# Inverse root by Ln and Exp on ScalarE, held weight transfers and deeper input buffers in an attention kernel

## The chip, the cores and the metric

The kernel runs on one core of a Trainium2 chip. The metric is the device time of one execution in microseconds. A core has five instruction streams that work side by side: TensorE (PE), VectorE (DVE), ScalarE (ACT), GpSimd (POOL) and SyncE (SP), each in the order of its own queue; transfers run on 16 DMA engines. Weight loads into TensorE have a row of their own in the profile (PEld), and "SPq" is SP's queue of transfers.

## The reference

Attention with normalised queries and keys over 8 batches, 12 heads, 448 positions and 64 channels, and then a two-layer network on the 3584 tokens:

```python
def rmsnorm(x, g):
    rms = np.sqrt(np.mean(x * x, axis=-1, keepdims=True) + 1e-06)
    return x / rms * g
q_n, k_n = (rmsnorm(q, g_q), rmsnorm(k, g_k))
scores = 1.0 / np.sqrt(64) * np.matmul(q_n, k_n.transpose(0, 1, 3, 2))
attn = softmax(scores)              # exp of (scores - max), over (sum + 1e-09)
x = np.matmul(attn, v)              # heads side by side: 3584 x 768
h = x @ w_in                        # 768 x 2048
out = (h * np.clip(h + 3.0, 0.0, 6.0) / 6.0) @ w_out    # 2048 x 768
```

## The kernel before

**Tiling.** A *pair* is two heads of one batch: 6 pairs per batch, 48 in all, counted by `P`. Of the 448 positions, 384 lie as three rows on each of 128 partitions (the pair's tiles); the other 64, the *rest rows*, are handled for all heads and two batches at once.

**One pair.** `load_pair` (L133) issues three transfers on SP: q and k into `qk` (L138), v into `vf` (L141). `prep_pair` (L146) makes the normalised rows on POOL: the squares `sq` (L150), their sums by 64 on DVE (`ssq`, L152), then `rstd_of` (L126): `ms`, mean plus epsilon (L128), and `rs`, that to the power -0.5 against a constant tile (L130). Two products give `qks` (L158) and a cast of v gives `va` (L164). `trans_pair` (L235) transposes `qks` on PE (L241), DVE copies q out to `qT` (L243) and k times the gains to `kp` (L247). `score` (L253) does one matmul and one exponential on ACT (`eT`, L264) per unit, seven per pair; `av` (L279) multiplies by the values, and DVE divides by the sum (`rd`, `xn`, L289, L291); `xtrans` (L324) transposes back. `load_rest`, `load_vrest`, `prep_rest` and `prep_vrest` (L170 to L208) do the same for the rest rows: `qkr` (L174), `vr` (L183), `vbd` (L190, POOL), `sqr` (L200), `qkrs` (L205). The scores of a batch need its rest rows, since `qT` holds all 448 positions.

**The network.** `h_part` (L341) multiplies by `w_in` (L349), ACT makes `t_sb` = relu(h/6 + 0.5) (L354), DVE takes min(t, 1) times h as `gT` (L356). `y_part` (L360) multiplies by `w_out` (L366), ACT copies to `y_sb` (L372), SP stores (L376, L380).

**Order.** The last loop (L464) merges the attention of batch b with the first layer of batch b-1 and the second layer of batch b-2; what is left of the network follows. Inside `att_items(P)` (L436) come the load of pair P+4, the preparation of P+3, the transposes of P+2, the scores of P+1 and the values of P. At the start (L449 to L462) four pairs are loaded, POOL issues the transfers of `w_in` (L452), three pairs are prepared, POOL issues those of `w_out` (L456), and the first scores follow. These positions are priorities: a planner in the framework simulates the engines, takes for each the ready instruction of highest priority and so fixes each queue's order beforehand; on the chip a queue then keeps that order. In the trace the squares of a pair stand several pairs ahead of its `qks`. A buffer is a limit to running ahead: four of `qk`, three of `vf`, four each of `ssq`, `ms`, `rs` and `qks`, two of `sq`, one of `qkr` (L99 to L104). A load into a `qk` buffer waits until the `qks` of the pair that held it is made; one into `vf`, for the cast.

Of the kernel before, what the change touches and what calls it, by code (L numbers as in the profile page):

```python
# [12 lines left out]
A_ADD = mybir.AluOpType.add  # L13
A_POW = mybir.AluOpType.pow
A_MIN = mybir.AluOpType.min
EXP = mybir.ActivationFunctionType.Exp
RELU = mybir.ActivationFunctionType.Relu
# [5 lines left out]
def kernel(  # L23
# [35 lines left out]
    for a in range(2):  # L59
        nc.sync.dma_start(out=gq_t[a * 64:(a + 1) * 64, :], in_=g_q.rearrange("(p o) -> p o", o=1))  # L60
        nc.sync.dma_start(out=gk_t[a * 64:(a + 1) * 64, :], in_=g_k.rearrange("(p o) -> p o", o=1))
    mask = const.tile([128, 2], FP32, name="mask")
# [5 lines left out]
    gmask = const.tile([128, 2], FP32, name="gmask")  # L68
    nc.vector.tensor_scalar(gmask[:], mask[:], gprime[:], 1.0 / 8.0, A_MULT, A_MULT)
    half_c = const.tile([128, 1], FP32, name="half_c")  # L70
    nc.gpsimd.memset(half_c[:], 0.5)
    zero_c = const.tile([128, 1], FP32, name="zero_c")
    nc.gpsimd.memset(zero_c[:], 0.0)
    npow = const.tile([128, 24], FP32, name="npow")
    nc.gpsimd.memset(npow[:], -0.5)

# [21 lines left out]

    qk_pool = pool("qk_pool", 4)  # L99
    v_pool = pool("v_pool", 3)  # L100
    sq_pool = pool("sq_pool", 2)
# [21 lines left out]
    st = {}  # L123


    def rstd_of(ssq, n):  # L126
        ms = st_pool.tile([128, n], FP32, name="ms", tag="ms")
        nc.gpsimd.tensor_scalar(ms[:], ssq, 1.0 / D, 1e-6, A_MULT, A_ADD)  # L128
        rs = st_pool.tile([128, n], FP32, name="rs", tag="rs")
        nc.gpsimd.tensor_tensor(out=rs[:], in0=ms[:], in1=npow[:, 0:n], op=A_POW)  # L130
        return rs

    def load_pair(P):  # L133
# [12 lines left out]
    def prep_pair(P):  # L146
        qk, vf = st.pop(("qk", P)), st.pop(("vf", P))
        sq = sq_pool.tile([128, 4 * NT * D], FP32, name="sq", tag="sq")
        qk_flat = qk[:].rearrange("p a h x -> p (a h x)")
        nc.gpsimd.tensor_tensor(out=sq[:], in0=qk_flat, in1=qk_flat, op=A_MULT)  # L150
        ssq = st_pool.tile([128, 4 * NT], FP32, name="ssq", tag="ssq")
        nc.vector.tensor_reduce(  # L152
            out=ssq[:], in_=sq[:].rearrange("p (n d) -> p n d", d=D), axis=AX_X, op=A_ADD)
        rs = rstd_of(ssq[:], 4 * NT)
        rs4 = rs[:].rearrange("p (a h t) -> p a h t", a=2, h=2)
        qks = qks_pool.tile([128, 2, NT, 2, D], BF16, name="qks")
        for i in range(2):
            nc.gpsimd.tensor_tensor(  # L158
                out=qks[:, i].rearrange("p t h d -> p h t d"),
                in0=qk[:, i].rearrange("p h (t d) -> p h t d", d=D),  # L160
                in1=rs4[:, i].unsqueeze(3).to_broadcast([128, 2, NT, D]),
                op=A_MULT)
        va = va_ring[P % NVA]
        nc.gpsimd.tensor_copy(  # L164
            out=va[:, :, :, 0:D], in_=vf[:].rearrange("p h (t d) -> p h t d", d=D))
        st["qks", P] = qks
        st["va", P] = va


    def load_rest(b):  # L170
        qkr = rst_pool.tile([128, 2, H, D], FP32, name="qkr")
        for i, src in enumerate((q, k)):
            for e in range(2):
                nc.sync.dma_start(  # L174
                    out=qkr[e * 64:(e + 1) * 64, i],
                    in_=src[b + e, :, SM:S, :].rearrange("h p d -> p h d"))
        st["qkr", b] = qkr
# [16 lines left out]
    def prep_rest(b):  # L194
        qkr = st.pop(("qkr", b))
        qks = rst_pool.tile([128, 2, H, D], BF16, name="qkrs")
        for i in range(2):
            sq = sq_pool.tile([128, 4 * NT * D], FP32, name="sqr", tag="sq")
            src = qkr[:, i].rearrange("p h d -> p (h d)")
            nc.gpsimd.tensor_tensor(out=sq[:], in0=src, in1=src, op=A_MULT)  # L200
            ssq = st_pool.tile([128, H], FP32, name="ssqr", tag="ssq")
            nc.vector.tensor_reduce(
                out=ssq[:], in_=sq[:].rearrange("p (n d) -> p n d", d=D), axis=AX_X, op=A_ADD)
            rs = rstd_of(ssq[:], H)
            nc.gpsimd.tensor_tensor(  # L205
                out=qks[:, i], in0=qkr[:, i],
                in1=rs[:].unsqueeze(2).to_broadcast([128, H, D]), op=A_MULT)
# [210 lines left out]
    def prep_step(P):  # L418
# [4 lines left out]
        if j == 0:  # L423
            if b % 2 == 0:
                prep_rest(b)
            prep_vrest(b)

    def trans_step(P):
# [7 lines left out]
    def att_items(P):  # L436
        b, j = divmod(P, NPAIR)
        n = P + 1
        items = [(0.0, lambda: load_step(P + 4)), (0.0, lambda: prep_step(P + 3)),
                 (0.36, lambda: trans_step(P + 2))]  # L440
# [7 lines left out]

    for P in range(4):  # L449
        load_step(P)  # L450
    for kt in range(NKT):
        nc.gpsimd.dma_start(out=w_in_sb[:, kt, :], in_=moe_w_in[kt * 128:(kt + 1) * 128, :])  # L452
    for P in range(3):
        prep_step(P)
    for ft in range(0, NFT, 4):
        nc.gpsimd.dma_start(  # L456
            out=w_out_sb[:, ft:ft + 4, :],
            in_=moe_w_out[ft * 128:(ft + 4) * 128, :].rearrange("(f p) n -> p f n", p=128))
    for P in range(2):
# [45 lines left out]
```

## Time and profile before

| | us |
|---|---|
| median of three runs | 673.85 |
| lowest and highest | 670.53, 674.61 |
| the profiled execution | 674.05 |
| its span (first to last instruction) | 672.3 |
| PE busy | 493.8 |
| POOL busy | 357.7 |
| ACT busy | 295.9 |
| DVE busy | 245.9 |

The profile is of one execution. Busy times count instructions at work, not transfers being issued. A row of a timeline gives the start, the duration, the engine, the source line, what is written from what, and in brackets how long the engine sat idle before it and what ended that.

### The profile page before, as it was taken

To read this page: it belongs to the slowest core of one execution; us is meant where nothing else is said; L and a number is where in the kernel's file an instruction comes from. 1 tells how busy PE (TensorE), PEld (TensorE's weight loads), DVE (VectorE), ACT (ScalarE), POOL (GpSimd) and SP (SyncE) were. 2 spreads that over 40 slices of the span, in tenths; PEclk is the share of its full clock that TensorE was granted. 3 is DMA by queue.
4 is the path that set the end of the run, shared out by engine and by line. 5 is a ranking of instruction groups with operands and counts; after the bars stand their busy time and mean duration, and the time that the engine had idled before them with its cause. 6 is when DMAs were issued, how large, how long until landed. Compare 5 with 4: busy or idle time off the path is not lost.

```text
span 672.3 us, 9839 instructions
## 1 busy us (share of the span) xinstructions
PE 493.8 (73%) x3848; PEld 290.1 (43%) x3848; DVE 245.9 (37%) x544; ACT 295.9 (44%) x521; POOL 357.7 (53%) x362
## 2 busy tenths in 40 slices
PE   0026354742869767978788868797879999999997
PEld 0013133421545434545454434464545556664454
DVE  0124223533645424334334423334444443433210
ACT  0006142531546434554345335464556666653321
POOL 2499699999796766546355684646455210000000
PEclk9999675877889978998789779999999999999999
DMA  8919733323331331222131212131222110101012
GB/s 154 232 43 198 147 100 85 93 59 83 89 83 49 93 90 53 86 79 61 58 83 49 71 47 71 59 95 60 84 59 71 48 37 25 36 24 36 24 47 72
DMA packets 69647, 50.98 MB, mean 76 GB/s; under 512 B 22752, under 2 KB 68832, under 8 KB 69600
## 3 DMA queue, kind: packets, MB, share of 16 engines
q1 hardware_dynamic: 66624, 44.06, 23.6%
q0 software_dynamic: 2976, 6.29, 5.2%
q8 instruction: 30, 0.49, 0.3%
q14 instruction: 17, 0.14, 0.1%
HBM read 45.61 MB, written 11.01 MB: 84 GB/s over the span
## 4 chain that ended last, share of the span: by engine, by line
POOL 35%; PE 30%; DMA 13%; DVE 8%; SPq 5%; issue 4%; ACT 3%; POOLq 0%; ACTq 0%
PE h_ps L349 13%; DMA qk<-in_k_dram 12%; PE y_ps L366 11%; POOL rs L130 11%; POOL sq L150 10%; POOL qks L158 8%; DVE ssq L152 4%; SPq L174 3%; PE s_ps L263 2%; ACT t_sb L354 2%; PE t_ps L241 2%; SPq L138 1%; POOL qkrs L205 1%; POOL ms L128 1%; DMA vr<-in_v_dram 1%
## 5 line engine op out<-in xcount | busy, mean ns | idle before, releaser
L264 ACT ACTIVATE eT<-s_ps,zero_c 128x448 bf16<-128x448 f32 x336 | 200.7, 634 | 117.9 <-PE s_ps L263 113.6
L354 ACT ACTIVATE t_sb<-h_ps,half_c 128x384 f32<-128x384 f32 (+1 forms) x128 | 81.0, 634 | 140.6 <-PE h_ps L349 136.2
L130 POOL TENSOR_TENSOR rs<-ms,npow 128x12 f32<-128x12 f32 x56 | 127.3, 2274 | 3.2
L150 POOL TENSOR_TENSOR sq<-qk 128x768 f32<-128x768 f32 x48 | 70.4, 1466 | 108.3 <-DMA qk<-in_k_dram 107.8
L349 PEld LDWEIGHTS <-w_in_sb 128*128 128x128 bf16 x768 | 75.0, 102 | 109.4 <-issue 70.6
L263 PE MATMUL s_ps<-qT,kp 128*128 128x448 bf16 x288 | 101.8, 384 | 9.5 <-DVE kp L247 4.3
L152 DVE TENSOR_REDUCE ssq<-sq 128x12 f32<-128x768 f32 x48 | 45.7, 951 | 170.8 <-POOL sq L150 170.8
L158 POOL TENSOR_TENSOR qks<-qk,rs 128x384 bf16<-128x384 f32 x96 | 77.5, 828 | 25.5 <-PE t_ps L241 24.6
L272 PEld LDWEIGHTS <-eT 128*128 128x128 bf16 x1152 | 69.1, 103 | 36.1 <-issue 8.5
L241 PE MATMUL t_ps<-identity,qks 128*128 128x128 bf16 x288 | 28.5, 240 | 68.6 <-POOL qks L158 51.8
L241 PEld LDWEIGHTS <-qks 128*128 128x128 bf16 x288 | 22.3, 107 | 80.4 <-POOL qks L158 54.2
L372 ACT COPY y_sb<-y_ps 128x384 f32<-128x384 f32 x56 | 26.8, 479 | 65.2 <-PE y_ps L366 65.1
L329 PE MATMUL xt_ps<-identity,xn 128*128 128x128 bf16 x144 | 19.1, 245 | 41.2 <-DVE xn L291 41.2
L263 PEld LDWEIGHTS <-kp 128*128 128x128 bf16 x288 | 29.3, 105 | 26.2 <-issue 7.9
L349 PE MATMUL h_ps<-xT_990,w_in_sb 128*128 128x512 bf16 x96 | 29.3, 423 | 12.2 <-DVE gT_1655 L356 11.7
L329 PEld LDWEIGHTS <-xn 128*128 128x128 bf16 x144 | 12.2, 109 | 53.9 <-DVE xn L291 47.4
L247 DVE TENSOR_SCALAR kp<-t_ps,gmask 128x384 bf16<-128x384 bf16 x96 | 35.2, 408 | 0.0
L349 PE MATMUL h_ps<-xT_2600,w_in_sb 128*128 128x512 bf16 x96 | 29.2, 420 | 6.9 <-DVE gT_3402 L356 6.4
L243 DVE COPY qT<-t_ps 128x384 bf16<-128x384 bf16 x48 | 17.0, 355 | 45.6 <-PE t_ps L241 45.4
L349 PE MATMUL h_ps<-xT_422,w_in_sb 128*128 128x384 bf16 x96 | 26.6, 376 | 7.1 <-DVE gT_905 L356 7.1
L349 PE MATMUL h_ps<-xT_1771,w_in_sb 128*128 128x384 bf16 x96 | 24.1, 363 | 9.8 <-DVE gT_2479 L356 9.6
L366 PE MATMUL y_ps<-w_out_sb,gT_1655 128*128 128x384 bf16 x128 | 29.1, 345 | 0.0
(102 smaller groups left out, 765.5 us busy)
## 6 DMA issues: line engine op xcount, KB each, us to landing
qk<-in_q_dram SPq DMA_DIRECT2D x48, 192.0 KB, 2.5
qk<-in_k_dram SPq DMA_DIRECT2D x48, 192.0 KB, 2.7
vf<-in_v_dram SPq DMA_DIRECT2D x48, 192.0 KB, 2.5
out_dram<-y_sb SPq DMA_DIRECT2D x48, 192.0 KB, 2.2
w_in_sb<-in_moe_w_in_dram POOLq DMA_DIRECT2D x6, 512.0 KB, 11.6
w_out_sb<-in_moe_w_out_dram POOLq DMA_DIRECT2D x4, 768.0 KB, 11.0
qkr<-in_q_dram SPq DMA_DIRECT2D x8, 192.0 KB, 3.8
qkr<-in_k_dram SPq DMA_DIRECT2D x8, 192.0 KB, 5.7
```

Source lines behind the costliest of these rows:

```text
L130: nc.gpsimd.tensor_tensor(out=rs[:], in0=ms[:], in1=npow[:, 0:n], op=A_POW)
L150: nc.gpsimd.tensor_tensor(out=sq[:], in0=qk_flat, in1=qk_flat, op=A_MULT)
L152: nc.vector.tensor_reduce(out=ssq[:], in_=sq[:].rearrange("p (n d) -> p n d", d=D), axis=AX_X, op=A_ADD)
L158: nc.gpsimd.tensor_tensor(out=qks[:, i].rearrange("p t h d -> p h t d"), in0=qk[:, i].rearrange("p h (t d) -> p h t d", d=D), in1=rs4[:, i ...
L241: nc.tensor.transpose(ps[:, i, t, :], qks[:, i, t].rearrange("p h d -> p (h d)"), identity[:])
L247: nc.vector.tensor_scalar_mul(kp[:, a, :], ps[:, 1].rearrange("p t c -> p (t c)"), gmask[:, a:a + 1])
L263: nc.tensor.matmul(out=ps[:], lhsT=lhsT, rhs=st["qT", b][:, j, :], start=True, stop=True)
L264: nc.scalar.activation(out=st["e", P][:, u, :], in_=ps[:], func=EXP, bias=zero_c[:], scale=1.0)
L272: nc.tensor.matmul(out=dst[:, a * E1:(a + 1) * E1], lhsT=eT[:, u, c0:c0 + 128], rhs=va[:, a, t, :], start=(first and a == 0 and t == 0), s ...
L349: nc.tensor.matmul(out=h_ps[:, 0:n], lhsT=w_in_sb[:, kt, f * 128:(f + 1) * 128], rhs=st["xT", G][:, kt, :], start=(kt == 0), stop=(kt == N ...
L354: nc.scalar.activation(out=t_sb[:, 0:n], in_=h_ps[:, 0:n], func=RELU, bias=half_c[:], scale=1.0 / 6.0)
L366: nc.tensor.matmul(out=y_ps, lhsT=gT[:, f, i * 128:(i + 1) * 128], rhs=w_out_sb[:, f, nh * HALF:(nh + 1) * HALF], start=(f == 0), stop=(f ...
```

## The change

- `rstd_of` becomes two instructions on ACT: Ln of the sum plus 64 x 1e-6, then Exp of -0.5 times that, in place. The two factors of 8 that this leaves out are put into `gmask` (times 8 instead of 1/8). One table set that holds both functions is loaded at the start; `npow` and `ms` are gone.
- The squares of pairs 0 to 2 and of the first rest rows are made on ACT, all others on POOL as before.
- The transfers of the gains and of the first batch's rest rows are issued by ACT instead of SP.
- `w_in` is issued from POOL's queue behind the cast of pair 1, `w_out` behind the cast of pair 6.
- `qk` has five buffers instead of four, `vf` four instead of three; five pairs are loaded at the start, and `att_items(P)` loads pair P+5.

```diff
-        nc.sync.dma_start(out=gq_t[a * 64:(a + 1) * 64, :], in_=g_q.rearrange("(p o) -> p o", o=1))
+        nc.scalar.dma_start(out=gq_t[a * 64:(a + 1) * 64, :], in_=g_q.rearrange("(p o) -> p o", o=1))
...
-    nc.vector.tensor_scalar(gmask[:], mask[:], gprime[:], 1.0 / 8.0, A_MULT, A_MULT)
+    nc.vector.tensor_scalar(gmask[:], mask[:], gprime[:], 8.0, A_MULT, A_MULT)
...
+    nc.gpsimd.memset(eps_c[:], D * 1e-6)
+    nc.scalar.preload_act_table_set("natural_log_exp_and_others")
...
-    qk_pool = pool("qk_pool", 4)
-    v_pool = pool("v_pool", 3)
+    qk_pool = pool("qk_pool", 5)
+    v_pool = pool("v_pool", 4)
...
     def rstd_of(ssq, n):
-        ms = st_pool.tile([128, n], FP32, name="ms", tag="ms")
-        nc.gpsimd.tensor_scalar(ms[:], ssq, 1.0 / D, 1e-6, A_MULT, A_ADD)
         rs = st_pool.tile([128, n], FP32, name="rs", tag="rs")
-        nc.gpsimd.tensor_tensor(out=rs[:], in0=ms[:], in1=npow[:, 0:n], op=A_POW)
+        nc.scalar.activation(out=rs[:], in_=ssq, func=LN, bias=eps_c[:])
+        nc.scalar.activation(out=rs[:], in_=rs[:], func=EXP, bias=zero_c[:], scale=-0.5)
         return rs
+
+    def square(out, x, early):
+        if early:
+            nc.scalar.square(out=out, in_=x)
+        else:
+            nc.gpsimd.tensor_tensor(out=out, in0=x, in1=x, op=A_MULT)
...
-        nc.gpsimd.tensor_tensor(out=sq[:], in0=qk_flat, in1=qk_flat, op=A_MULT)
+        square(sq[:], qk_flat, P < 3)
...
-        nc.gpsimd.tensor_copy(
+        st["prep", P] = nc.gpsimd.tensor_copy(
...
-                nc.sync.dma_start(
+                (nc.scalar if b == 0 else nc.sync).dma_start(
...
-            nc.gpsimd.tensor_tensor(out=sq[:], in0=src, in1=src, op=A_MULT)
+            square(sq[:], src, b == 0)
...
+        if P == NPAIR:
+            load_w_out()
...
-        items = [(0.0, lambda: load_step(P + 4)), (0.0, lambda: prep_step(P + 3)),
+        items = [(0.0, lambda: load_step(P + 5)), (0.0, lambda: prep_step(P + 3)),
...
+    def load_w_in():
+        for kt in range(NKT):
+            after(nc.gpsimd.dma_start(
+                out=w_in_sb[:, kt, :], in_=moe_w_in[kt * 128:(kt + 1) * 128, :]), st["prep", 1])
...
+    def after(x, y):
+        tc.add_manual_dep(
+            x.ins, y.ins.name,
+            mybir.DependencyInfo(mybir.DependencyClass.NoSync, mybir.DependencyReason.DATA),
+            reason="transfers of weights follow the first inputs")
+
-    for P in range(4):
+    for P in range(5):
         load_step(P)
-    for kt in range(NKT):
-        nc.gpsimd.dma_start(out=w_in_sb[:, kt, :], in_=moe_w_in[kt * 128:(kt + 1) * 128, :])
     for P in range(3):
         prep_step(P)
...
+        if P == 1:
+            load_w_in()
```

`load_w_out` has the same form, behind `st["prep", NPAIR]`. `after` sets an order inside POOL's queue and no wait between engines.

## Rows read from the trace of the kernel before

**Rows 1.** Windows by stage: stretch, length, busy per engine, PEclk, DMA share, GB/s
```profile
48.20:125.40 77.20, 41.06 (x338) 24.69 (x338) 26.84 (x63) 32.26 (x57) 69.44 (x69) 0.73 0.57 126
125.40:189.70 64.30, 37.42 (x327) 23.83 (x326) 29.55 (x70) 28.38 (x52) 58.05 (x55) 0.81 0.28 76
189.70:271.30 81.60, 62.81 (x458) 34.57 (x458) 32.09 (x66) 37.35 (x64) 58.16 (x53) 0.88 0.27 76
...
423.30:494.20 70.90, 58.59 (x506) 36.69 (x504) 30.34 (x70) 36.48 (x66) 37.46 (x38) 0.98 0.25 76
494.20:552.30 58.10, 56.01 (x461) 32.14 (x459) 25.92 (x59) 37.24 (x64) 20.55 (x25) 1.00 0.18 54
552.30:606.30 54.00, 53.74 (x476) 33.87 (x474) 21.34 (x53) 32.66 (x59) 1.02 (x2) 1.00 0.09 29
606.30:672.30 66.00, 58.55 (x317) 30.83 (x316) 11.52 (x17) 17.61 (x30) 0.00 (x0) 0.99 0.14 46
```

**Rows 2.** Waits view: who waited for whom, us in total, times, longest
```profile
DVE ssq L152 <- POOL sq L150: 170.8, 44, 11.2
```

**Rows 3.** Timeline, 270 to 285 us, one pair's loop: start, us, engine, line
```profile
272.48 1.62 POOL L158 TENSOR_TENSOR qks<-qk,rs 128x384 bf16<-128x384 f32 x2 [1.64 <-PE t_ps L241]
...
274.54 0.46 SPq L138 DMA_DIRECT2D qk<-in_k_dram  x1
...
277.21 1.47 POOL L150 TENSOR_TENSOR sq<-qk 128x768 f32<-128x768 f32 x1 [3.11 <-DMA qk<-in_k_dram]
...
278.71 0.95 DVE L152 TENSOR_REDUCE ssq<-sq 128x12 f32<-128x768 f32 x1 [1.65 <-POOL sq L150]
...
279.75 0.20 POOL L128 TENSOR_SCALAR ms<-ssq 128x12 f32<-128x12 f32 x1 [1.08 <-DVE ssq L152]
280.04 2.30 POOL L130 TENSOR_TENSOR rs<-ms,npow 128x12 f32<-128x12 f32 x1
...
282.29 0.51 POOL L164 CAST va_89<-vf 128x384 bf16<-128x384 f32 x1
...
282.76 1.61 POOL L158 TENSOR_TENSOR qks<-qk,rs 128x384 bf16<-128x384 f32 x2
```

**Rows 4.** Timeline, 0 to 75 us, from the first loads to the scores
```profile
6.60 16.31 SPq L174 DMA_DIRECT2D qkr<-in_k_dram  x2
...
20.64 1.47 POOL L150 TENSOR_TENSOR sq<-qk 128x768 f32<-128x768 f32 x1 [15.16 <-DMA qk<-in_k_dram]
...
48.19 0.91 PE L263 MATMUL s_ps<-qT,kp 128*128 128x448 bf16 x2 [4.08 <-DVE qT L226]
```

**Rows 5.** Groups by form: count | busy us, mean ns | idle before
```profile
L130 POOL TENSOR_TENSOR rs<-ms,npow 128x12 f32<-128x12 f32 x56 | 127.3, 2274 | 3.2
...
L354 ACT ACTIVATE t_sb<-h_ps,half_c 128x512 f32<-128x512 f32 x64 | 44.0, 687 | 77.6 <-PE h_ps L349 77.4
L354 ACT ACTIVATE t_sb<-h_ps,half_c 128x384 f32<-128x384 f32 x64 | 37.0, 580 | 63.0 <-PE h_ps L349 58.8 <-DVE rd L289 4.2
...
L190 POOL TENSOR_SCALAR vbd_96<-vr,mask 128x384 bf16<-128x384 f32 x6 | 7.5, 1252 | 0.1
...
L452 POOL DMA_DIRECT2D w_in_sb<-in_moe_w_in_dram x6 | 3.5, 585 | 0.2 <-issue 0.2
L456 POOL DMA_DIRECT2D w_out_sb<-in_moe_w_out_dram x4 | 3.3, 820 | 0.1
```

**Rows 6.** Windows view of the head, columns as in rows 1
```profile
14.00:18.00 4.00, 0.00 (x0) 0.00 (x0) 0.00 (x0) 0.00 (x0) 0.00 (x0) 1.00 1.06 221
...
22.00:24.00 2.00, 0.00 (x0) 0.00 (x0) 0.95 (x1) 0.00 (x0) 0.61 (x2) 1.00 1.35 202
...
28.00:30.00 2.00, 0.00 (x0) 0.00 (x0) 0.00 (x0) 0.00 (x0) 1.25 (x1) 1.00 1.10 325
```

**Rows 7.** Timeline of POOL after the second set of weights was issued
```profile
76.31 1.47 POOL L150 TENSOR_TENSOR sq<-qk 128x768 f32<-128x768 f32 x1 [5.61 <-DMA qk<-in_k_dram]
```

**Rows 8.** Timeline, ACT's one table load
```profile
48.81 1.28 ACT L264 ACT_TABLE_LOAD   x1 [48.81 <-PE s_ps L263]
```

More of the change, by code (lines that the diff above doesn't have):

```diff
@@ L13 @@
 A_ADD = mybir.AluOpType.add
-A_POW = mybir.AluOpType.pow
 A_MIN = mybir.AluOpType.min
+LN = mybir.ActivationFunctionType.Ln
 EXP = mybir.ActivationFunctionType.Exp
@@ L59 @@
     for a in range(2):
-        nc.sync.dma_start(out=gq_t[a * 64:(a + 1) * 64, :], in_=g_q.rearrange("(p o) -> p o", o=1))
-        nc.sync.dma_start(out=gk_t[a * 64:(a + 1) * 64, :], in_=g_k.rearrange("(p o) -> p o", o=1))
+        nc.scalar.dma_start(out=gq_t[a * 64:(a + 1) * 64, :], in_=g_q.rearrange("(p o) -> p o", o=1))
+        nc.scalar.dma_start(out=gk_t[a * 64:(a + 1) * 64, :], in_=g_k.rearrange("(p o) -> p o", o=1))
     mask = const.tile([128, 2], FP32, name="mask")
@@ L73 @@
     nc.gpsimd.memset(zero_c[:], 0.0)
-    npow = const.tile([128, 24], FP32, name="npow")
-    nc.gpsimd.memset(npow[:], -0.5)
+    eps_c = const.tile([128, 1], FP32, name="eps_c")
+    nc.gpsimd.memset(eps_c[:], D * 1e-6)
+    nc.scalar.preload_act_table_set("natural_log_exp_and_others")
     w_in_sb = const.tile([128, NKT, DFF], BF16, name="w_in_sb")
@@ L447, in att_items, with load_w_out @@
         return items
-    for P in range(4):
+    def load_w_in():
+        for kt in range(NKT):
+            after(nc.gpsimd.dma_start(
+                out=w_in_sb[:, kt, :], in_=moe_w_in[kt * 128:(kt + 1) * 128, :]), st["prep", 1])
+    def load_w_out():
+        for ft in range(0, NFT, 4):
+            after(nc.gpsimd.dma_start(
+                out=w_out_sb[:, ft:ft + 4, :],
+                in_=moe_w_out[ft * 128:(ft + 4) * 128, :].rearrange("(f p) n -> p f n", p=128)),
+                st["prep", NPAIR])
+    def after(x, y):
[4 more added lines that the diff above has]
+    for P in range(5):
         load_step(P)
-    for kt in range(NKT):
-        nc.gpsimd.dma_start(out=w_in_sb[:, kt, :], in_=moe_w_in[kt * 128:(kt + 1) * 128, :])
     for P in range(3):
         prep_step(P)
[L455 to L458, printed above, removed]
+        if P == 1:
+            load_w_in()
     for P in range(2):
```

## The prediction

> **What bounds the kernel now.** The page's first part shows no engine that is busy all the time, but its shares are averages over unlike stages. So I read the windows view next, with the span cut at the first score and then at the hardswish products of one batch after another [rows 1]. The reader is to see three regimes. In the first two stages (attention of batch 0, then attention of batch 1 with the first layer of batch 0) POOL is busy 69.44 of 77.20 us and 58.05 of 64.30 us, PE little over half, at a granted clock of 0.73 and 0.81: POOL is the bound. From 189.70 to 494.20 no engine is full, and a stage takes 70.90 to 81.60 us. In the last stage with attention, 552.30 to 606.30, POOL has nothing left (1.02 us), PE is busy 53.74 of 54.00 us at full clock: that is what such a stage costs when only PE limits it.
>
> What fills the middle stages is shown by the waits and one pair's loop in the timeline. DVE waited 170.8 us, 44 times, for POOL's squares [rows 2], 3.9 us each. The loop [rows 3]: `qks` frees an input buffer (272.48, 1.62 us), SP issues the next load (274.54), POOL sits idle 3.11 us until it has landed, squares it (277.21), DVE sums (278.71), POOL does `ms` and the power (280.04, 2.30 us), the cast, and only then the next `qks` at 282.76. That is 10.28 us, more than the 9.0 us per pair of the PE-bound stage (54.00/6). DVE works in order, so its wait for the squares also holds the hardswish product behind it, and that holds PE's next matmuls.
>
> The head is the third loss. The first scores run at 48.19 [rows 4], because the first inputs, issued before 6.60, reach POOL only at 20.64 behind the 3 MB of `w_in`, and SP stood 16.31 us over two transfers of rest rows; then come the squares, powers and scalings of POOL in a row.
>
> **The change, part by part.**
>
> *Ln and Exp for the power.* POOL loses 56 powers of 2.274 us [rows 5] and 56 `ms` of 0.20 us [rows 3]: 138.6 us. The trace has no such small ACT instruction. Two ends: `t_sb` takes 687 ns at 512 columns and 580 ns at 384 [rows 5], so 0.84 ns per column, and 12 columns come to 580 - 372 x 0.84 = 0.27 us; the far end is the 0.580 itself; below nothing is excluded, they are instructions ACT did not have. I take 0.27, since the line goes through two forms of one engine: 112 x 0.27 = 30 us, 3.8 us per batch. ACT is busy 32.66 of 54.00 us in the PE-bound stage, so the time hides there; in the first attention stage ACT has 32.26 of 77.20 us.
>
> The loop of [rows 3] becomes: `qks` 1.62, then to the squares 3.1, squares 1.47, cast 0.51, next `qks`: 6.7 us instead of 10.28, under PE's 9.0. POOL is then in time, and what is late next is PE. What stays is DVE's wait: even where POOL itself had waited for PE before `qks` (the 1.64 us at 272.48), DVE sat idle 1.65 us before the sums (278.71). The stage 494.20 to 552.30 has two of the six squares left in it and took 4.1 us more than the last: 2.0 us per pair. I put 0.9 us per pair, half of 1.65 and less than 2.0 because the power is gone from it. A middle stage: 54.0 + 6 x 0.9 = 59.5 us. Ends: 54.0, and 70.9 (the best middle stage of before).
>
> *Deeper buffers* (five and four instead of four and three, loads one pair earlier). The framework's planner fills queues as far ahead as buffers allow, so the next load is still issued when a `qks` or a cast ends; I cost it at nothing. It gives slack for late transfers if the sums sit further behind in DVE's queue; then the 0.9 goes, 22 us at most over four stages.
>
> *Weights held, gains and rest rows issued on ACT.* The first input is now issued ahead of the gains and meets no weights. Until pair 4 and the rest rows are in, some 3.9 MB move: 5 pairs of 0.59 MB, rest rows 0.79 MB, their values 0.2 MB. The transfers of pairs moved 325 GB/s at best (28 to 30 us), the stretch with rest rows 202 GB/s [rows 6], so 12 to 19 us for all, and about 12 for the rest rows, which the first score needs. ACT issues these 8 transfers before its squares, while it has nothing else to do.
> On this the Trainium skill (DMA: Bandwidth & Descriptors, "Issuing engines are not separate DMA queues") says that another issuing engine saves only the issue time, since all transfers share the same 16 engines; by it the rest rows would land with the last of the 3.9 MB, at about 19, and the sum below would be 7 us higher. The trace bears half of it out: SP's 16.31 us over two issues did hold the loads behind them.
>
> *First squares on ACT.* Five, of 0.687 + 256 x 0.00084 = 0.90 us by the same line, while ACT is idle, instead of 1.47 us each on POOL. After the rest rows' landing: square 0.9, sum 0.95, Ln and Exp 0.6, two scalings 1.47 each, transposes and copies 2: about 8 us. First score at 12 + 8 = 20 us instead of 48.19; ends 16 and 27.
>
> *First stage.* POOL's work for six pairs is 6 x (1.47 + 1.62 + 0.51) = 21.6 us, plus 2 x 1.25 for the values' rest rows [rows 5], plus issuing the weights, 3.5 + 3.3 us [rows 5], which used to lie mostly in the idle head: 31 us. ACT has 32.26 + 3.8. Weights, held until the cast of pair 1, now arrive inside this stage: 3 MB at 221 GB/s are 14 us, twice. Before, the second set cost POOL a wait of 5.61 us [rows 7]. I take 40 us; ends 32 and 57 (77.20 less eight powers and `ms`). *Second stage:* 64.30 less 8 x 2.47 = 44.5, since POOL bound it; ends 38 and 54.
>
> The waits added (Ln on the sums, POOL's scaling on Exp, weights on casts) sit ahead of score exponentials on ACT; ACT has 21 us free per PE-bound stage, and with four `rs` buffers Ln follows an earlier `qks`, so I cost them at nothing and carry the other case below.
>
> **Sum**, against the profiled execution (span 672.30, 674.05 with what lies around it, 0.2 us above the median of 673.85): head 20 + 40 + 44.5 + four middle stages 4 x 59.5 = 238 + 56 (half of the 4.1 us of that stage gone) + 54 + tail 66 [rows 1] = 518.5, and 1.75 around the span: 520 us.
>
> **The rivals.**
> *A. POOL is freed, but DVE's wait stays.* The planner spends the deeper buffers on running ahead, every sum again stands right behind its load, and the squares' landing still sets the pace. For it: in-order DVE and 44 waits of 3.9 us; against it: the wait was 1.65 where POOL was in time. Middle stages at 70.9: 520 + 4 x 11.4 = 566.
> *B. Weights choke the first stages.* Pair loads behind 14 us of weights, twice, with the five loaded pairs covering one of them. For it: the 5.61 us on POOL [rows 7]; against it: deeper buffers. First two stages 10 us longer each: 540.
> *C. The table is not kept.* If Ln and Exp came from two tables, 2 x 56 loads of 1.28 us [rows 8] would stand in ACT's queue: 143 us, of which about 85 would show (ACT has 21 us free per stage and pays 18 to 19 there, but each load stands ahead of waiting scores): 605. Against it: the one load in before and the explicit pin.
> The Trainium skill (ScalarE: Activation LUTs, "Table sets: the hidden batching unit") lists one set that holds both functions, and a switch between sets at about 2.66 us with its drain, which would make 298 us of the 143; no run so far shows the drain.
> *D. ACT becomes the in-order bottleneck (slower).* If Ln is queued right behind a pair's last score exponential, ACT waits out the whole way from `qks` to the finished sum, 274.10 to 279.66 = 5.56 us, each pair, and then does its own 37.3/6 + 0.63 = 6.85 us: 12.4 us per pair. 48 x 12.4 + 20 + 66 + 1.75 = 683. It decides from a stall of 5.4 us per pair on. Against it: POOL squares well ahead of need, and the planner sees the dependency.
>
> **How the numbers follow.** About 1% is what a measurement of this kernel tells from no change. Forecast (POOL off the path, 59.5 per middle stage) 0.50; A 0.24; B 0.14; C 0.06; D 0.06. The predicted time is 520. With 54.0 for each middle stage and the short ends of head and first stages it is 520 - 22 - 4 - 8 = 486; a mix of the forecast with partly better overlap seldom gets below 490. Upward the range takes in B and A, with A's head late by 7 and a first stage at 54: 590. Left out: C and D, 0.12, and a little at the low end. D gives slower (0.05) or about the same; C at its far end the same: faster 0.93, same 0.02, slower 0.05.
>
> **What would show it.** First score at 16 to 27 us; no power on POOL, its busy time down by 140 us or more; one table load; 112 small ACT instructions of 0.2 to 0.6 us; DVE's wait for squares below 80 us in total; middle stages at 54 to 64 us at a clock near 1.0; the last two parts unchanged at 54 and 66. Middle stages still above 68 would prove me wrong for A, a first stage above 50 with POOL waiting on loads for B, a long ACT wait on the sums for D.

## The result, and the profile after

The changed kernel takes 581.11 us (median of four runs, 579.25 to 584.54) against 674.23 us of the kernel before in the same runs: a ratio of 0.8632, interval 0.8574 to 0.8691. The direction is right and the time lies in the range, but it is 61 us above the predicted 520 us. The profiled execution has a span of 582.8 us. Its page begins with the busy times, for the engines of the table of before:

```profile
PE 469.9 (81%) x3848; PEld 278.2 (48%) x3848; DVE 245.7 (42%) x544; ACT 320.5 (55%) x638; POOL 212.9 (37%) x245
```

POOL lost 144.8 us and ACT gained 24.6; DVE stayed.

Next, the span cut as in [rows 1]: at the first score, at the first hardswish product of batch 0, and then at the last one of each batch from 0 to 6 (differences of the starts, in us; S1 and S2 are the first two stages, S3 to S6 the four middle ones):

| | head | S1 | S2 | S3 | S4 | S5 | S6 | S7 | S8 | tail |
|---|---|---|---|---|---|---|---|---|---|---|
| before | 48.2 | 77.2 | 64.3 | 81.7 | 75.8 | 76.2 | 71.0 | 58.1 | 54.0 | 66.0 |
| predicted | 20 | 40 | 44.5 | 59.5 | 59.5 | 59.5 | 59.5 | 56 | 54 | 66 |
| after | 39.3 | 40.0 | 43.3 | 72.9 | 72.4 | 69.2 | 67.5 | 58.2 | 54.0 | 66.0 |

The windows view of the kernel after has the rows that answer to [rows 1]: stretch, length, busy time of PE, PEld, DVE, ACT and POOL, granted clock, DMA share, GB/s.

```profile
39.30:79.30 40.00, 31.63 (x337) 20.06 (x337) 23.53 (x60) 31.55 (x68) 35.43 (x41) 0.91 0.84 172
79.30:122.60 43.30, 33.79 (x334) 21.10 (x331) 31.32 (x70) 33.41 (x79) 37.76 (x38) 0.92 0.64 166
122.60:195.50 72.90, 57.53 (x461) 32.46 (x458) 34.28 (x69) 41.39 (x84) 35.79 (x37) 0.98 0.35 93
...
267.90:337.10 69.20, 57.79 (x461) 32.72 (x459) 30.98 (x64) 40.49 (x80) 28.96 (x30) 0.98 0.23 69
337.10:404.60 67.50, 59.01 (x507) 36.66 (x505) 30.39 (x71) 38.94 (x78) 22.19 (x25) 0.97 0.25 77
404.60:462.80 58.20, 55.96 (x461) 32.28 (x460) 25.15 (x58) 37.86 (x68) 14.21 (x19) 1.00 0.14 44
462.80:516.70 53.90, 53.65 (x474) 33.83 (x472) 21.26 (x52) 32.71 (x59) 1.02 (x2) 1.00 0.08 28
```

The reader is to see that POOL's load fell everywhere, and that only the first two stages took the whole benefit of it. In the middle stages POOL is busy 22 to 36 us, no engine is full, and still a stage takes 67 to 73 us.

The groups by form of the kernel after show the new instructions and the one table load (count, busy us, mean ns, idle before).

```profile
L131 ACT ACTIVATE rs<-rs,zero_c 128x12 f32<-128x12 f32 x56 | 17.8, 317 | 0.7
...
L130 ACT ACTIVATE rs<-ssq,eps_c 128x12 f32<-128x12 f32 x48 | 15.0, 313 | 51.9 <-POOL qks L165 37.3 <-DVE gT_1641 L363 5.5 <-DVE ssq L159 4.0
...
L136 ACT ACTIVATE sq<-qk 128x768 f32<-128x768 f32 x3 | 2.5, 832 | 8.6 <-DMA qk<-in_q_dram 8.6
...
L77 ACT ACT_TABLE_LOAD x1 | 1.3, 1283 | 3.3 <-issue 3.3
```

The waits view has what became of [rows 2] (who waited for whom, us in total, times, longest).

```profile
DVE ssq L159 <- POOL sq L138: 87.3, 37, 5.5
POOL sq L138 <- DMA qk<-in_k_dram: 80.6, 25, 4.7
...
POOL qks L165 <- PE t_ps L248: 71.1, 24, 4.8
...
ACT rs L130 <- POOL qks L165: 39.2, 24, 4.4
```

DVE's wait for the squares was halved, from 170.8 us, and did not go. How it sets the pace is seen in the chain of work that ended last, traced through 24 us of a middle stage (start, duration, what; `issue` steps are left out).

```profile
268.59 1.62 POOL qks L165 x2
...
270.65 2.60 DMA qk<-in_k_dram
...
273.42 1.47 POOL sq L138
...
274.92 0.95 DVE ssq L159
...
276.00 0.56 DVE xn L298
276.56 0.61 DVE gT_3374 L363
...
277.21 1.45 PE h_ps L356 x6
278.66 0.35 PE t_ps L248 x6
...
279.15 1.63 POOL qks L165 x2
```

That is a closed loop of 279.15 - 268.59 = 10.56 us per pair. A `qks` frees an input buffer, the load that waited for it starts at once, its squares follow the landing, and the planner has put their sum at that very place in DVE's queue. Behind the sum stand `xn` and the hardswish product `gT`, PE's next `h_ps` needs that, the transposes `t_ps` of the next pair stand behind `h_ps`, and the next `qks` waits for `t_ps` to give up a buffer. Where squares of rest rows are due too, a turn takes longer: the next is 291.86 - 279.15 = 12.71 us. The mean of the middle stages, 281.9 / 24 = 11.7 us per pair, lies between these two.

The loop is not new. The same view of the kernel before shows the turn just ahead of the one in [rows 3]:

```profile
258.34 0.80 POOL qks L158
...
264.32 0.95 DVE ssq L152
265.28 0.61 DVE gT_1655 L356
...
272.06 0.35 PE t_ps L241 x6
...
272.48 1.63 POOL qks L158 x2
```

It takes 14.1 us and goes over DVE and PE with no power in it; the turn after it closes on POOL, through the power [rows 3]. The change took away the second way and left the first.

Last, the head, in the timeline of the kernel after (start, us, engine, line, what; in brackets the idle time before and its end).

```profile
8.10 5.04 ACTq L181 DMA_DIRECT2D qkr<-in_k_dram  x2
...
11.38 2.91 POOL L460 DMA_DIRECT2D w_in_sb<-in_moe_w_in_dram  x5
...
15.88 13.13 SPq L190 DMA_DIRECT2D vr<-in_v_dram  x4
32.71 0.84 ACT L136 ACTIVATE sqr<-qkr 128x768 f32<-128x768 f32 x1 [17.30 <-DMA vr<-in_v_dram]
33.46 0.29 ACT L131 ACTIVATE rs<-rs,zero_c 128x12 f32<-128x12 f32 x1
...
33.84 1.62 POOL L165 TENSOR_TENSOR qks<-qk,rs 128x384 bf16<-128x384 f32 x2 [19.55 <-DMA vr<-in_v_dram]
...
39.30 0.91 PE L270 MATMUL s_ps<-qT,kp 128*128 128x448 bf16 x2 [0.45 <-DVE qT L233]
```

The weights did not wait for the first inputs. They are held behind the cast of pair 1, and that cast needs `v` alone; it ran at 10.94, and five of the six transfers of `w_in` left from 11.38 on, when the second half of the rest rows' keys, issued at 12.53, was not yet under way. It landed at 32.61, and the second `sqr` ran at 32.71. The profile names `vr` as what ended that wait, but the instruction reads `qkr`: the name goes by the event that came last. ACT works in order, so the Exp of pair 0 (33.46), whose sum had been ready since 15, stood behind that square, and with it the first `qks`.

### The profile page after: what moved, and what is told of

Same layout as the page of the kernel before. It is cut to its first block, busy times and chain, and to the rows that moved or that the text cites. A ratio compares the mean times of both kernels' runs of the same rounds, so it can differ in the third digit from the quotient of the medians.

```text
span 582.8 us, 9889 instructions
## 1 busy us (share of the span) xinstructions
PE 469.9 (81%) x3848; PEld 278.2 (48%) x3848; DVE 245.7 (42%) x544; ACT 320.5 (55%) x638; POOL 212.9 (37%) x245
## 3 DMA queue, kind: packets, MB, share of 16 engines
q1 hardware_dynamic: 63168, 43.27, 26.4%
## 4 chain that ended last, share of the span: by engine, by line
PE 35%; POOL 23%; DMA 19%; DVE 10%; ACT 5%; issue 4%; SPq 4%; POOLq 0%; ACTq 0%
DMA qk<-in_k_dram 15%; PE h_ps L356 14%; PE y_ps L373 13%; POOL qks L165 9%; POOL sq L138 9%; DVE ssq L159 4%; ACT t_sb L361 3%; PE s_ps L270 3%; SPq L190 2%; PE t_ps L248 2%; SPq L145 2%; POOL sqr L138 1%; DMA vr<-in_v_dram 1%; DMA qkr<-in_k_dram 1%; DVE xn L298 1%
## 5 line engine op out<-in xcount | busy, mean ns | idle before, releaser
L356 PEld LDWEIGHTS <-w_in_sb 128*128 128x128 bf16 x768 | 72.5, 98 | 95.5 <-issue 54.9
L270 PE MATMUL s_ps<-qT,kp 128*128 128x448 bf16 x288 | 97.1, 360 | 2.5 <-DVE kp L254 1.3
L138 POOL TENSOR_TENSOR sq<-qk 128x768 f32<-128x768 f32 x45 | 66.0, 1468 | 88.4 <-DMA qk<-in_k_dram 80.6
L159 DVE TENSOR_REDUCE ssq<-sq 128x12 f32<-128x768 f32 x48 | 45.7, 952 | 95.7 <-POOL sq L138 87.3
L279 PEld LDWEIGHTS <-eT 128*128 128x128 bf16 x1152 | 66.3, 100 | 30.4 <-issue 2.5
L248 PE MATMUL t_ps<-identity,qks 128*128 128x128 bf16 x288 | 26.1, 228 | 44.6 <-POOL qks L165 41.1
L379 ACT COPY y_sb<-y_ps 128x384 f32<-128x384 f32 x56 | 26.8, 479 | 44.0 <-PE y_ps L373 43.9
L130 ACT ACTIVATE rs<-ssq,eps_c 128x12 f32<-128x12 f32 x48 | 15.0, 313 | 51.9 <-POOL qks L165 37.3
L356 PE MATMUL h_ps<-xT_984,w_in_sb 128*128 128x512 bf16 x96 | 26.6, 394 | 11.3 <-DVE gT_1641 L363 10.7
L356 PE MATMUL h_ps<-xT_2580,w_in_sb 128*128 128x512 bf16 x96 | 26.5, 389 | 6.9 <-DVE gT_3374 L363 6.7
L373 PE MATMUL y_ps<-w_out_sb,gT_1641 128*128 128x384 bf16 x128 | 28.0, 338 | 1.7 <-ACT y_sb L379 1.6
L373 PE MATMUL y_ps<-w_out_sb,gT_3374 128*128 128x384 bf16 x128 | 27.3, 332 | 1.7 <-ACT y_sb L379 1.6
L356 PE MATMUL h_ps<-xT_1757,w_in_sb 128*128 128x384 bf16 x96 | 22.0, 337 | 7.9 <-DVE gT_2459 L363 7.8
L250 DVE COPY qT<-t_ps 128x384 bf16<-128x384 bf16 x48 | 17.0, 355 | 26.6 <-PE t_ps L248 26.4
L298 DVE TENSOR_TENSOR xn<-x_ps,rd 128x384 bf16<-128x384 f32 x48 | 26.7, 555 | 1.2
```

Source lines behind the costliest of these rows:

```text
L138: nc.gpsimd.tensor_tensor(out=out, in0=x, in1=x, op=A_MULT)
L159: nc.vector.tensor_reduce(out=ssq[:], in_=sq[:].rearrange("p (n d) -> p n d", d=D), axis=AX_X, op=A_ADD)
L248: nc.tensor.transpose(ps[:, i, t, :], qks[:, i, t].rearrange("p h d -> p (h d)"), identity[:])
L270: nc.tensor.matmul(out=ps[:], lhsT=lhsT, rhs=st["qT", b][:, j, :], start=True, stop=True)
L279: nc.tensor.matmul(out=dst[:, a * E1:(a + 1) * E1], lhsT=eT[:, u, c0:c0 + 128], rhs=va[:, a, t, :], start=(first and a == 0 and t == 0), s ...
L298: nc.vector.tensor_tensor(out=xn[:], in0=xv[:, :, :, 0:D], in1=rd[:].unsqueeze(3).to_broadcast([128, NT, 2, D]), op=A_MULT)
```

## The experiments

Each kernel was timed beside the kernel before. The table has the profiled execution cut as above (us) and the median; the ratio is to the kernel before on the same chip, and kernels are compared by it where little lies between them.

| kernel | first score | end of S2 | S3 to S6 together | span | median | ratio and interval |
|---|---|---|---|---|---|---|
| before | 48.2 | 189.7 | 304.6 | 672.3 | 674.23 | |
| after | 39.3 | 122.6 | 281.9 | 582.8 | 581.11 | 0.8632 (0.8574 to 0.8691) |
| e1_pow | 38.5 | 171.8 | 293.4 | 643.6 | 646.10 | 0.9589 (0.9544 to 0.9633) |
| e2_bufs4 | 37.6 | 132.4 | 284.9 | 598.4 | 597.76 | 0.8851 (0.8800 to 0.8902) |
| e3_qk8 | 38.1 | 126.7 | 260.3 | 564.1 | 566.81 | 0.8401 (0.8360 to 0.8442) |
| e5_st8 | 38.4 | 122.6 | 286.4 | 587.4 | 587.45 | 0.8702 (0.8666 to 0.8738) |
| e7_pin | 39.0 | 117.9 | 225.8 | 519.7 | 521.11 | 0.7726 (0.7701 to 0.7752) |
| e12_before_pin | 48.3 | 163.3 | 239.8 | 579.3 | 580.64 | 0.8601 (0.8554 to 0.8649) |
| e4_hold | 28.3 | 123.0 | 273.5 | 574.6 | 578.43 | 0.8585 (0.8536 to 0.8635) |
| e10_nohold | 41.3 | 136.4 | 272.9 | 587.4 | 594.27 | 0.8798 (0.8750 to 0.8846) |
| e11_sqpool | 32.0 | 117.0 | 281.0 | 576.2 | 576.99 | 0.8557 (0.8522 to 0.8593) |
| e9_pin_hold | 28.8 | 113.4 | 225.8 | 515.1 | 516.71 | 0.7656 (0.7620 to 0.7692) |
| e13_best | 26.4 | 109.8 | 225.8 | 511.5 | 514.25 | 0.7620 (0.7583 to 0.7657) |

### The power back on POOL

The kernel after, with `rstd_of` as it was:

```diff
-        nc.scalar.activation(out=rs[:], in_=ssq, func=LN, bias=eps_c[:])
-        nc.scalar.activation(out=rs[:], in_=rs[:], func=EXP, bias=zero_c[:], scale=-0.5)
+        nc.gpsimd.tensor_scalar(ms[:], ssq, 1.0, D * 1e-6, A_MULT, A_ADD)
+        nc.gpsimd.tensor_tensor(out=rs[:], in0=ms[:], in1=npow[:, 0:n], op=mybir.AluOpType.pow)
```

> The changed kernel with the inverse root back on POOL (one add and one power per pair, the same factors), all else as changed. Theory (the power on POOL is what held the first two stages, and a part of the middle ones): POOL gets 56 x 2.47 = 138 us back, the two first stages return towards 77 and 64 us from 40 and 43 (+58), the middle stages gain some 20 in all; total 640 to 665 against 581. Rival (held weights and deeper buffers carried most of the 93 us, the power was hidden): total at most 620, with the first two stages below 55 us each.

646.10 us, so Ln and Exp are worth 65 us of the 93, with all else as changed. The windows view of this kernel, first two stages:

```profile
38.50:102.90 64.40, 36.18 (x338) 23.35 (x338) 25.95 (x62) 32.06 (x58) 62.54 (x63) 0.73 0.50 108
102.90:171.80 68.90, 41.90 (x330) 25.24 (x331) 30.17 (x70) 27.67 (x50) 61.50 (x57) 0.75 0.39 102
```

POOL is full again in S1 (62.54 of 64.40 us) and nearly so in S2. Of the 60.8 us between the spans, 24.4 + 25.6 = 50 lie in these two stages and only 293.4 - 281.9 = 11.5 in the four middle ones, where the forecast had expected 66.6 (304.6 less 4 x 59.5).

### The buffers: one fewer, three more, and more for the sums

`e2_bufs4` goes back to the buffers of before:

```diff
-    qk_pool = pool("qk_pool", 5)
-    v_pool = pool("v_pool", 4)
+    qk_pool = pool("qk_pool", 4)
+    v_pool = pool("v_pool", 3)
...
-        items = [(0.0, lambda: load_step(P + 5)), (0.0, lambda: prep_step(P + 3)),
+        items = [(0.0, lambda: load_step(P + 4)), (0.0, lambda: prep_step(P + 3)),
...
-    for P in range(5):
+    for P in range(4):
```

> The changed kernel with four and three input buffers and loads of pair P+4 again. Theory (a deeper buffer is spent on running ahead, the load still follows the product that frees the buffer, so one buffer more buys nothing by itself): middle stages stay at 67 to 74 us, total 578 to 590. Rival (the fifth buffer carried a good part of the gain): middle stages back to 71 to 82, total 600 or more.

597.76 us, between the two. The middle stages hardly move (284.9 against 281.9); S1 is 14.0 us longer (54.0 against 40.0), S2 2.6 shorter. The waits view of S1 in this kernel:

```profile
POOL sq L138 <- DMA qk<-in_k_dram: 11.6, 1, 11.6
```

That one wait is for keys issued while the transfers of `w_out` were under way. With the deeper buffers POOL waits for no load in S1. So the deeper buffers pay once, where the weights stand in the way, and hardly in the loop of the middle.

`e3_qk8` gives `qk` eight buffers (`qk_pool = pool("qk_pool", 8)`), nothing else.

> The changed kernel with eight qk buffers instead of five; ssq and rs keep four. Theory 1 (the middle stages are held by a loop: product frees a buffer, load, squares, sums, and DVE's queue stands behind the sums): with eight buffers against four of ssq and rs the load and the squares are done long before the sums may be written, so DVE's wait for POOL's squares falls from 87 us to under 40, the four middle stages from 72.9, 72.4, 69.2 and 67.5 us to 58 to 63, total 535 to 555. Theory 2 (ACT's Ln waiting for the product that frees an rs buffer, 39.2 us in all, holds them): the middle stages stay within 2 us, total 575 to 585.

566.81 us, short of the hoped-for range. The waits view of this kernel:

```profile
DVE ssq L159 <- POOL sq L138: 41.3, 21, 3.5
...
ACT rs L130 <- POOL qks L165: 37.1, 27, 2.1
```

Three more buffers halve DVE's wait again, and the middle stages fall by 21.6 us. They do not end it: with the input buffers plentiful, DVE still waits 41.3 us for squares and ACT's Ln 37.1 us for a `qks` to free an `rs` buffer. Whether the limit has passed to the next pool is not shown: no run has eight buffers of both.

`e5_st8` asks whether that second wait costs anything by itself: five buffers of `qk` as in the change, but eight each of `ssq` and `rs` (`st_pool = pool("st_pool", 8)`).

> The changed kernel with eight buffers each for ssq and rs instead of four, five qk buffers kept. Theory 2 (ACT's Ln waits for the product that frees an rs buffer, 39.2 us in the changed kernel and 37.1 with eight qk buffers, and its queue stands behind it): that wait goes and the middle stages fall by 4 us or more each, total 560 to 572. Theory 1 (the squares' load, made only when a product frees the buffer, holds DVE): the wait of ACT moves from the product to the sums, DVE's wait stays at 80 to 100 us, middle stages stay within 3 us, total 575 to 590.

587.45 us, no gain. The waits view of this kernel:

```profile
DVE ssq L159 <- POOL sq L138: 89.3, 37, 6.2
...
ACT rs L130 <- DVE ssq L159: 46.9, 28, 4.1
```

ACT's Ln no longer waits for a `qks`; it waits for the sum instead, rather longer than before (46.9 us), and DVE's wait stands. Ln's wait was cover for another one, and costs nothing that shows here.

### The order of the sums

If the place of the sum in DVE's queue makes the loop, a place further back must open it, with all buffers as they are. `e7_pin` puts the sum of pair P behind the copy of the transposed result (`xT`) of pair P-4, where the program's own order has it. Both are on DVE, so no wait between engines is added.

```diff
-        nc.vector.tensor_reduce(
+        red = nc.vector.tensor_reduce(
...
+        if P >= 4:
+            after(red, st["xtc", P - 4])
...
-        nc.vector.tensor_copy(
+        st["xtc", P] = nc.vector.tensor_copy(
```

> The changed kernel with one order more: the sums of pair P stand in DVE's queue behind the copy of pair P-4's attention output (no wait between engines, no buffer changed). So the planner can't put the sums ahead of their program place, and a load has several pairs of time. Theory 1 (middle stages are held by DVE standing behind sums whose load has just been issued): DVE's wait for POOL's squares falls below 30 us, the four middle stages to 55 to 60 us each, total 525 to 545. Theory 2 (ACT behind Ln) or a third cause (PE's own pace with an attention and two network layers is 67 to 73 us when all preparations run): middle stages within 4 us of 72.9, 72.4, 69.2 and 67.5, total 565 to 585.

521.11 us, better than the range of the theory. The windows view of two middle stages, two lines of its waits, and its timeline around one sum:

```profile
173.95:230.60 56.65, 56.08 (x493) 35.54 (x492) 31.32 (x73) 40.20 (x82) 29.19 (x31) 1.00 0.40 109
230.60:287.10 56.50, 55.97 (x473) 32.74 (x472) 29.75 (x65) 41.10 (x77) 23.98 (x27) 1.00 0.30 88
```

```profile
POOL sq L138 <- DVE ssq L159: 46.1, 25, 2.6
...
DVE ssq L159 <- POOL sq L138: 1.7, 1, 1.7
```

```profile
248.17 0.35 DVE L339 COPY xT<-xt_ps 128x384 bf16<-128x384 bf16 x1
...
248.43 0.94 DVE L159 TENSOR_REDUCE ssq<-sq 128x12 f32<-128x768 f32 x1
...
249.46 1.47 POOL L138 TENSOR_TENSOR sq<-qk 128x768 f32<-128x768 f32 x1 [1.89 <-DVE ssq L159]
```

DVE's wait is 1.7 us in all, once. It is POOL that now waits, for the sum to free a `sq` buffer, and POOL has the time: it is busy 24 to 29 us of 56.5. PE is busy 55.97 of 56.50 us at clock 1.00, so it is the bound at last, and ACT's 112 new instructions lie under it. The middle stages lost 56.1 us by an edit of the order alone. With the sums pinned the planner also orders POOL, ACT and PE anew, so the 56.1 us are the price of the early sums with what follows from them, not of DVE's queue by itself.

`e12_before_pin` makes the same edit in the kernel before, with its power on POOL, its four buffers and its weights first.

> The kernel before, nothing of the change, with only the order of e7_pin: the sums of pair P behind the copy of pair P-4's attention output in DVE's queue. Theory 1 alone (the middle stages were held by the early sums from the start, and POOL's 44.5 us per batch, power included, fit under PE's 54): the middle stages fall from 81.6, 75.8, 76.2 and 71.0 us to 55 to 62, the first two stay near 77 and 64; total 590 to 615. Rival (the power on POOL is needed off the way as well): middle stages stay at 68 us or more, total 640 or more.

580.64 us, below the range of the theory: the order alone gives the kernel before as much as the whole change does (0.8601 against 0.8632). The windows view of its stages S1 to S4:

```profile
48.35:112.68 64.33, 37.12 (x332) 22.31 (x332) 23.56 (x59) 30.67 (x54) 57.32 (x59) 0.76 0.65 139
...
112.70:163.30 50.60, 38.69 (x346) 24.00 (x343) 28.87 (x68) 30.15 (x56) 46.37 (x44) 0.83 0.33 87
163.30:220.30 57.00, 55.79 (x463) 32.35 (x462) 29.72 (x64) 37.85 (x65) 42.14 (x42) 1.00 0.32 95
220.30:283.30 63.00, 57.74 (x494) 36.12 (x492) 31.39 (x73) 36.45 (x66) 49.05 (x47) 0.97 0.35 97
```

In the middle stages, with most of the wait gone (20.2 us of 170.8 are left), the power hides under PE in S3 and S5 (57.0 and 56.9 us). What it costs can show in S4 and S6 alone (63.0 and 62.9), where POOL also has the rest rows of two batches; how these hold PE was not traced. Over the four stages this kernel is 14.0 us longer than `e7_pin` (239.8 less 225.8), which has the rest of the change too. In the middle stages of the kernel before it was the order of the sums, far more than the power, that cost time: 304.6 less 239.8, or 64.8 us.

The total came out below the range because the first two stages did not stay, as the theory had it: S1 fell from 77.2 to 64.3 us and S2 from 64.3 to 50.7, with the power still on POOL. POOL has 57.32 us of work in S1 instead of 69.44 [rows 1]: in the early order it made 11 powers in S1 and 10 in S2, some of them for later pairs, and now it makes eight in each. So a part of what bound these two stages was the order as well. Between `e12_before_pin` and `e7_pin` lie 59.6 us of span, 45.4 of them up to the end of S2; how they divide between the power, the buffers and the held weights with the order in place, no run separates.

### The head: where the weights are held, and who squares

`e4_hold` ties `w_in` to the scaling of the first rest rows instead of the cast of pair 1:

```diff
-            nc.gpsimd.tensor_tensor(
+            st["rest", b] = nc.gpsimd.tensor_tensor(
...
-                out=w_in_sb[:, kt, :], in_=moe_w_in[kt * 128:(kt + 1) * 128, :]), st["prep", 1])
+                out=w_in_sb[:, kt, :], in_=moe_w_in[kt * 128:(kt + 1) * 128, :]), st["rest", 0])
```

> The changed kernel with w_in tied to the last product of the first rest rows (the second qkrs) instead of the cast of pair 1, which only needs v. Theory (w_in was released at 11.4 us, ahead of the rest rows' transfers, and these then landed at about 32): the first score comes at 20 to 25 us instead of 39.3, the first attention stage is 40 to 46 us, total 563 to 573. Rival (the transfers are only shifted: pair loads of the first stages wait behind w_in then, and the first product of w_in is late): what the head gains the first two stages lose, total 577 to 586.

578.43 us, as the rival had it. The timeline of this kernel:

```profile
18.75 0.84 ACT L136 ACTIVATE sqr<-qkr 128x768 f32<-128x768 f32 x1 [3.74 <-DMA qkr<-in_k_dram]
```

The mechanism of the head is shown: without weights beside them the rest rows are squared at 18.75 instead of 32.71, and the first score runs 11 us earlier. But the weights then come inside S1 and take it back: S1 is 48.7 us instead of 40.0, and S2 ends at 123.0 instead of 122.6. The 8.2 us by which this span is shorter lie in the middle stages, which the edit does not touch; what shortened them was not tried. The two medians differ by 2.7 us, and the intervals of the ratios overlap.

`e10_nohold` takes the hold away: `load_w_in()` stands before the loop of `prep_step`, `load_w_out()` behind it, both without `after`.

> The changed kernel with the weights' transfers issued as before the change: w_in at once, w_out behind the first three preparations, no order to any cast. Theory (w_in at 11.4 us still comes ahead of half the rest rows, so the hold gains little in the head, and it puts w_out's transfers into the first stage): total within 6 us of 581. Rival (the hold is what brought the first score from 48.2 to 39.3 us and more): first score at 46 to 50 us, total 588 to 596.

594.27 us, in the rival's range, yet by neither reason in full: the first score is at 41.3, only 2 us later. S1 is longer, 55.6 instead of 40.0 us. The hold as written is worth 11 us by the ratios and 13 by the medians, and it is the first stage that it helps. In the profiled executions S2 (39.5 against 43.3 us) and the middle stages (272.9 against 281.9) give most of that back, so the two spans differ by 4.6 us only. The windows view of S1 without the hold has PE at a clock of 0.72 and POOL busy 45.88 us:

```profile
41.30:96.90 55.60, 37.45 (x338) 23.32 (x338) 26.92 (x62) 33.33 (x69) 45.88 (x49) 0.72 0.78 172
```

`e11_sqpool` leaves all squares on POOL (`if early:` becomes `if False:`).

> The changed kernel with the first squares on POOL again. Theory (ACT and POOL both wait for the rest rows' transfers in the head; five squares cost POOL 5 x 1.47 us, of which what follows the landing at 32 us shows): first score 1 to 4 us later, total 581 to 586. Rival (ACT works in order: its second square of rest rows waited 17.3 us for a transfer with pair 0's Exp queued behind it, so squares on POOL set pair 0 free earlier): first score at 39 us or before, total 574 to 581.

576.99 us; by the median the squares on ACT cost 4 us instead of saving something, though the intervals of the ratios just overlap. The timeline of this kernel:

```profile
14.89 1.61 POOL L165 TENSOR_TENSOR qks<-qk,rs 128x384 bf16<-128x384 f32 x2 [0.54 <-ACT rs L131]
...
26.38 1.47 POOL L138 TENSOR_TENSOR sqr<-qkr 128x768 f32<-128x768 f32 x1 [8.45 <-DMA qkr<-in_k_dram]
```

The first `qks` runs at 14.89 instead of 33.84, since nothing that waits for the rest rows stands ahead of its Exp on ACT. But the squares, being in POOL's queue, also delay the weights behind them: three transfers of `w_in` instead of five are issued before the rest rows' keys have landed, and the second `sqr` runs at 26.38 instead of 32.71. The first score comes 7.3 us earlier and S2 ends 5.6 us earlier. 6.3 of the 7.3 us are the earlier landing, and only about 1 us is left for the Exp of pair 0.

### Together

`e9_pin_hold` is `e7_pin` with the edit of `e4_hold`; `e13_best` is that with the edit of `e11_sqpool`.

> e7_pin and e4_hold together. Theory (they act in different places: the order in the middle, the hold in the head, where e4_hold brought the first score 11 us forward and gave 8.7 of it back in the first stage): total 2 to 6 us below the 521 of e7_pin, 514 to 520. Rival (with the sums kept in place the loads have slack, so the first stage no longer gives it back): total 508 to 514.

> e9_pin_hold with the first squares on POOL again. Theory (on ACT pair 0's Exp stands behind a square that waits for the rest rows' keys, and e11_sqpool alone had its first score 7.3 us earlier): total 3 to 8 us below e9_pin_hold. Rival (with w_in held behind the rest rows' products the two gains are the same one): within 2 us of e9_pin_hold.

516.71 and 514.25 us. The second is 2.5 us below the first, between what the theory and its rival expected, and the intervals overlap. Both beat the two kernels of the case: `e13_best` is 0.7620 (0.7583 to 0.7657) of the kernel before. Here the weights are held behind the rest rows in both, and the first score still comes 2.4 us earlier with the squares on POOL: that is what their place costs without the weights. With the middle in order, the earlier head keeps some of its gain: S2 ends at 109.8 instead of the 117.9 of `e7_pin`.

## Why the prediction was right or wrong

The profiled span is 64.3 us above the predicted sum of 518.5. By the first table, 19.3 of it lie in the head, 43.9 in the four middle stages (281.9 less 238) and 2.2 in S7; S2 gives back 1.2. The two misses have two causes. That the time lies in the range at all is not the forecast's merit: the range took in rival A with a late head. Rival A's 566 us with the 19.3 of the head come to 585, against 584.54 in the profiled execution.

**The middle stages: wrong, and it was rival A.** The step that failed is "POOL is then in time, and what is late next is PE", with its 0.9 us per pair. It counted the loop of [rows 3] as one that closes on POOL, so that taking out the power would bring 10.28 us down to 6.7, under PE's 9.0. The loop closes through DVE's queue, the product, PE's `h_ps` and `t_ps` back to `qks`, and takes 10.56 us without any power. The measured stages exceed the PE-bound one by (281.9 / 4 - 54.0) / 6 = 2.7 us per pair, three times the 0.9. By the prediction's own signs it was A: three of the four stages are above 68 us, and DVE's wait is 87.3 us, above 80. The rows for it were there: the prediction itself names DVE's in-order wait and the product behind it, then takes POOL's wait for PE ahead of `qks` in [rows 3], 1.64 us, as a sign that POOL was in time, where it was the same loop coming round (258.34 to 272.48). Rival A had 70.9 for these stages and 566 in all; measured are 70.5 on the mean and 581. Its words "every sum again stands right behind its load" are what the chain shows; `e7_pin` moves the sums and takes 56.1 us off, which settles it. The floor of 54.0 us was a little low too: with the loop open and PE full, a middle stage takes 56.5 us.

**Deeper buffers: costed at nothing, right in the middle, wrong in S1.** `e2_bufs4` shows 3 us in S3 to S6 and 14.0 us in S1. The 22 us "if the sums sit further behind" needed another means: one buffer more does not open the loop, three more (`e3_qk8`) gain 21.6 us, and an order 56.1.

**The head: wrong.** The step that failed is "about 12 for the rest rows": the last of them landed at 32.6. Without the weights they land at about 19 (`e4_hold`), so some 7 us of the miss are the 12 itself and 14 the early release. The rest of that term held: from the second `sqr` to the first score it is 39.30 - 32.71 = 6.6 us, for 8 predicted. The weights "held until the cast of pair 1" were read as held until the first inputs were in; the cast needs only `v`, and ran at 10.94. And of the squares on ACT "while ACT is idle" only the duration was asked, not what stands behind them: the Exp of pair 0 did, which cost the head 1 us (`e11_sqpool`) to 2.4 (`e13_best`).

On this the Trainium skill (DMA: Bandwidth & Descriptors, "Issuing engines are not separate DMA queues") was cited: another engine saves only the issue. The runs agree with it: the rest rows, issued by ACT, did not pass SP's and POOL's transfers, and where no weights were among them (`e4_hold`) their last square ran at 18.75, close to the 19 that the prediction worked out by that rule and set aside. Its remark that the issue time is usually small beside the transfer does not hold here: SP stood 13.13 us over four issues.

**The first two stages: right in size.** 40.0 for 40 and 43.3 for 44.5. POOL bound them, and `e1_pow`, where it again does, takes 64.4 and 68.9. The terms behind the sizes were not right: the kernel before made 11 and 10 powers in these stages, not eight, and with the order of the sums alone, power and all, they take 64.3 and 50.7 us (`e12_before_pin`). The 40 is not right by its terms alone: part of the weights came in the longer head, and `e4_hold`, with weights where the forecast had them, shows 48.7. There rival B's 10 us come nearly true for S1, and not in the change.

**The sizes.** Ln and Exp took 0.313 and 0.317 us for 0.27 predicted: 48 x 0.313 + 8 x 0.319 + 56 x 0.317 = 35 us instead of 30. ACT's square took 0.83 for 0.90. POOL's busy time fell from 357.7 to 212.9, by 144.8 us; the 138.6 predicted and five squares of 1.47 make 146. ACT's busy time rose by only 24.6, less than the 39 us of its new instructions, since the records of neighbouring ACT instructions overlap (the Exp at 33.46 takes 0.29, and the next Ln starts at 33.66). All of these are small.

**The added waits: right in price.** Ln waited 39.2 us for `rs` buffers, and `e5_st8`, which takes that wait away, is no faster. Rival D has the wait on the sums at 4.0 us in all, not 5.4 per pair. Rival C fell with one table load of 1283 ns.

**S7, S8 and the tail: right**, 58.2, 54.0 and 66.0; half of S7's 4.1 us was expected to go, and stayed.

## What to carry to other kernels

A wait on a faster producer need not go when the producer gets faster: follow what stands behind the waiting instruction round to what starts the producer, and if the loop closes, change the place of the wait in the queue before buying buffers or engine time for it. An order that is to hold transfers back must hang on the last of the inputs that it protects, and an early instruction moved to an idle in-order engine must be asked what will stand behind it while it waits. A gain in the head is only a gain once it is still there at the end of the next stages.

## What the runs showed that was not expected

The edit of the order is worth as much on the kernel before as a change of five parts; once DVE hardly waited, only 14.0 us in the four middle stages separated the kernel with the 2.3 us power from the one with the whole change.

PE's time for the same work moved with the stalls. In S1 it was busy 41.06 us for 338 matmuls at a granted clock of 0.73 before [rows 1], and 31.63 us for 337 at 0.91 after, where its idle time in the stage was 8.4 us instead of 36.1; without the hold it is 37.45 at 0.72, with 18.2 us idle. These clocks are means over stretches at 1.2 and 2.4 GHz. In the middle stages of `e7_pin`, where PE hardly idles, it is 1.00 throughout. So where POOL's stall went, PE's own work took less time as well.

Kernels that differ only in the head had middle stages of 273 to 282 us (`e4_hold`, `e10_nohold`, `e11_sqpool`, the change); the three with the sums pinned and the change otherwise have 225.8. The planner's order differs a little between the unpinned ones, and the two shorter ones have a granted clock of 0.99 over these stages where the change has 0.97. What makes the 9 us was not tried.
